# Stage 0 of a mixer layer: v first, phi folded in 64x64 tiles, and fp32 work gathered in shared runs

## The chip, the cores and the metric

The kernel runs on one core of a Trainium2 chip. The metric is the device time of one execution in microseconds; before the change it is 649.45 us, the median of three runs (648.33 to 650.24).

## What is computed

Input x is 2048 rows of 512. With xn = layernorm(x), the output is x + A(xn) + B(xn).

```python
# A: linear attention, 32 heads of 16
q, k, v = split(xn @ wqkv)
pq, pk = q @ w_phi[h], k @ w_phi[h]                      # per head
phi_q = concat(softmax(pq), softmax(-pq)); phi_k likewise
kv = phi_k^T v;  z = sum_s phi_k
A = (phi_q kv / (phi_q z + 1e-6)) @ wo
# B: gated MLP with a mix over the rows
z1, z2 = split(gelu(xn @ w_in)); z2 = layernorm(z2)
B = (z1 * (w_sp @ z2 + b_sp)) @ w_out
```

## The kernel before

Rows are taken in 16 tiles of 128 (NT). Stage 0, the first third of the time, makes k's features and the kv sum, q's features (sent to DRAM) and most of z1 before its gelu (sent to DRAM). Stage 1 makes z2, then comes w_sp @ z2, then the output projections. Only stage 0 is touched.

Most matmuls take fp32 data split in a high and a low part, both of a reduced fp32 format ("fp32r"): `mm3` (L49) issues high x high, high x low and low x high, at L51, L52 and L53. `round_h` (L41, ScalarE) makes the high part and `rest_l` (L46, VectorE) the low part. A projection of a tile to 512 columns is 12 such matmuls (`proj`, L213), z1 of a tile 24 of 344 columns (`zproj`, L122). Other matmuls run in plain fp32, and each is two records in the profile: the transposes of x (L248, one record each), the fold (L197) and the kv sum (L273).

The fold replaces q's and k's weights by their product with w_phi, so that a projection gives pq or pk straight away. `phi_bd` is w_phi as four block-diagonal 128x128 matrices (eight heads each). `fold` (L194) multiplies each 128x128 block of the transposed weights with it; `folded` (L201) splits the result into `wqk_h` and `wqk_l`.

Per tile s, stage 0 does this. `stats` (L232) takes mean and variance on VectorE, and POOL derives the rest. `center` (L241, ScalarE) subtracts the mean, `transposed` and `split_x` (L244, L226) turn the tile and split it, giving `xT[s]`. `proj_k` (L260) projects, and `softmax_pair` (L100) makes both softmaxes: two reductions (max, min), two subtractions, an exponential on ScalarE, a sum and a reciprocal. `add_kv` (L267) normalises the features on VectorE, adds them into `zacc` by a DMA, and multiplies them with v into one PSUM bank (16 matmuls on column tiles of 32, L271 to L274). `proj_v` (L255) and `proj_q` (L263) are the other projections; q lags by some tiles, and z1 (`z1_raw`, L136) by more.

What sets the order: the framework's planner orders each engine's instructions at build time, by its own estimate of when each is ready, earlier-written ones first. `tc.issue_after(i)` keeps the instructions that are written inside it, on i's engine, behind i. In the head (L296 to L339) `keep` puts nearly all into a fixed order: a table load and eleven idle transposes, statistics of tile 0, fold of k, splits of k's weights and of v's, k of tile 0, v of tile 0, fold of q in two halves. The loop (L341 to L357) is left to the planner. SP issues the loads in the order written (L276 to L282); x tiles go through five buffers (`XB`), and so do the eight pieces of w1 (`load_win`, L208).

Of the kernel before, what the change touches and what calls it, by code (L numbers as in the profile page):

```python
# [35 lines left out]
def mixer(ctx: ExitStack, tc: tile.TileContext, x, x_t, wv, wqkT, phi_bd, wo, w_in, wst, b_r, w_out, out):  # L36
# [63 lines left out]
    def softmax_pair(pl, src, tag, scale=1.0, ebufs=2):  # L100

        mm = pl.tile([P, 2, H], F32, tag=tag + "mm", bufs=1, name="mm")
        dve.tensor_reduce(mm[:, 0], heads(src), axis=AX.X, op=ALU.max)
# [4 lines left out]
        dve.tensor_tensor(e2[:, :, 0], heads(src), bc(mm[:, 0], H), op=ALU.subtract)  # L108
        dve.tensor_tensor(e2[:, :, 1], bc(mm[:, 1], H), heads(src), op=ALU.subtract)  # L109
        act.activation(e, e, AF.Exp, scale=scale)  # L110
        sm = pl.tile([P, 2 * H], F32, tag=tag + "sm", bufs=1, name="sm")
        dve.tensor_reduce(sm, heads(e), axis=AX.X, op=ALU.add)  # L112
        dve.reciprocal(r, sm)
        return er
# [7 lines left out]
    def zproj(ps, s, w, order=(0, 1)):  # L122
# [7 lines left out]
        for k, j in enumerate(order):  # L130
            for c in range(ND):
                cs = slice(c * P, (c + 1) * P)
                mm3(p[k][:, :FC], (t[:, 0, cs], t[:, 1, cs]), (w[j][0][:, c], w[j][1][:, c]), c == 0, c == ND - 1)
# [7 lines left out]

    LAG = 5
    xT = []
# [17 lines left out]
    with ExitStack() as p0:  # L161
# [16 lines left out]
        def split_w(h, l, src, t):  # L178
            sp.dma_start(t, src)
            round_h(act, h, t)  # L180
            rest_l(l, t, h)

        bd = stage("bd")[:, 0, :D]

        def load_rows(src, x_at={}):
            raw = [stage("wrow") for _ in range(2)]
            parts = [raw[c // 2][:, c % 2, :D] for c in range(ND)]
            for c in range(ND):
                if c in x_at:
                    fetch(x_at[c])  # L190
                sp.dma_start(parts[c], src[c * P:(c + 1) * P, :])
            return parts

        def fold(wT, g, accs):  # L194
            gs = slice(g * P, (g + 1) * P)
            for c, acc in accs:
                ins = pe.matmul(acc[:, gs], wT[g][:, c * P:(c + 1) * P], bd[:, gs], start=g == 0, stop=g == NG - 1,  # L197
                                skip_group_check=True).ins
            return ins

        def folded(i, accs, keep=lambda **ins: None):  # L201
            for c, acc in accs:
                keep(act=round_h(act, wqk_h[:, i, c], acc))
                keep(dve=rest_l(wqk_l[:, i, c], acc, wqk_h[:, i, c]))

        w1 = [[w1_pool.tile([P, ND, FC], F32R, name=f"w1_{j}{k}") for k in "hl"] for j in range(2)]

        def load_win(dst, j, stp, tag, bufs):  # L208
            for c in range(ND):
                t = stp.tile([P, D if tag == "x" else FC], F32, tag=tag, bufs=bufs, name="wst_")  # L210
                split_w(dst[0][:, c], dst[1][:, c], w_in[c * P:(c + 1) * P, j * FC:(j + 1) * FC], t[:, :FC])

        def proj(s, wh, wl):  # L213
            p = ps.tile([P, D], F32, tag="mm", name="proj")
            for c in range(ND):
                cs = slice(c * P, (c + 1) * P)
                proj.last = mm3(p, (xT[s][:, 0, cs], xT[s][:, 1, cs]), (wh[:, c], wl[:, c]), c == 0, c == ND - 1)
# [14 lines left out]
        def stats(s):  # L232
            st6 = wk.tile([P, 6], F32, tag="st6", name="st6")
            dve.bn_stats(st6, xt[s])
            nm = wk.tile([P, 1], F32, tag="nm", name="nm")
            ins = dve.bn_aggr(mv_x[:, s], st6).ins
            pool.tensor_scalar_mul(nm, mv_x[:, s, 0:1], -1.0)
            rstd_of(mv_x[:, s], r_x[:, s:s + 1])
            return nm, ins

        def center(s, nm):  # L241
            return act.activation(xt[s], xt[s], AF.Identity, bias=nm).ins
# [8 lines left out]
        def centered(s):  # L251
            center(s, stats(s)[0])
            split_x(transposed(s)[0])

        def proj_v(s):  # L255
            v[s] = wk.tile([P, D], F32, tag="v", name="v")
            ins = act.activation(v[s], proj(s, wv_h, wv_l), AF.Copy, scale=r_x[:, s:s + 1]).ins
            return proj.last, ins

        def proj_k(s):  # L260
            return softmax_pair(wk, proj(s, wqk_h[:, 1], wqk_l[:, 1]), "k", r_x[:, s:s + 1])
# [5 lines left out]
        def add_kv(s, er):  # L267
            vs, e = v.pop(s), er[:, :NF]
            dve.tensor_tensor(heads(e), heads(e), bc(er[:, NF:], 2 * H), op=ALU.mult)
            pool.dma_start(zacc, e, accum_op=ALU.add)  # L270
            for m in range(H // 2):  # L271
                k = m % 4 * QP
                pe.matmul(kv_acc[k:k + QP, m // 4], vs[:, m * QP:(m + 1) * QP], e[:, m * HP:(m + 1) * HP],  # L273
                          start=s == 0 and m < 4, stop=s == NT - 1, skip_group_check=True)  # L274

        sp.dma_start(bd, phi_bd.rearrange("p g f -> p (g f)"))  # L276
# [12 lines left out]
        def warm_up(n):  # L289

            t = ps.tile([P, ND, P], F32, tag="mm", name="idle")
            for k in range(n):
                i = pe.transpose(t[:, k % ND], ident, ident).ins
            keep(pe=i)

        with ExitStack() as queue:  # L296
            tbl = wk.tile([P, 1], F32, tag="nm", name="tbl")
            keep(act=act.activation(tbl, mhalf, AF.Identity, bias=mhalf).ins)
            warm_up(11)
            nm, i = stats(0)  # L300
            keep(dve=i, act=center(0, nm))
            accs = [(c, (za, kv_ps_p)[c // 2].tile([P, D], F32, tag="z", name="fold")) for c in range(ND)]
            for g in range(NG):
                if g == NG - 1:
                    pt, i = transposed(0)
                    keep(pe=i)
                keep(pe=fold(wkT, g, accs))
            i, j = split_x(pt)
            keep(act=i, dve=j)
            nm, i = stats(1)  # L310
            keep(dve=i)
# [3 lines left out]
            keep(act=center(1, nm))  # L315
            for c in range(ND):
                keep(act=round_h(act, wv_h[:, c], wvr[c]))
                keep(dve=rest_l(wv_l[:, c], wvr[c], wv_h[:, c]))
            p = proj(0, wqk_h[:, 1], wqk_l[:, 1])
            keep(pe=proj.last)  # L320
            pt, i = transposed(1)
            keep(pe=i)
            i, j = split_x(pt)
            keep(act=i, dve=j)
            nm, i = stats(2)
            keep(dve=i, act=center(2, nm))
            ek = softmax_pair(wk, p, "k", r_x[:, 0:1])
            keep(pe=proj_v(0)[0])
            for k in range(2):
                accs = [(2 * k + m, za.tile([P, D], F32, tag="z", name="fold")) for m in range(2)]  # L330
                for g in range(NG):
                    i = fold(wqT, g, accs)
                folded(0, accs)
                if k == 0:
# [4 lines left out]
                    proj_v(1)  # L339
        n1 = nq = 0  # L340
        for s in range(NT):  # L341
            fetch(s + 4)
            er = proj_k(s) if s else ek
            if 0 < s < NT - 2:
                centered(s + 2)
            while nq < (s - 2) * NT // (NT - 3):
                proj_q(nq)
                nq += 1
            add_kv(s, er)
            if s + 2 < NT:  # L350
                proj_v(s + 2)
# [82 lines left out]
    with ExitStack() as p1:  # L434
# [27 lines left out]
        with ExitStack() as p1a:  # L462
            ta = p1a.enter_context(left("tmp1a", 1))
            for j in range(2):
                load_win(w2[j], 2 + j, ta, "st", 4)
# [406 lines left out]
```

## Time and profile before

| | us |
|---|---|
| median of 3 runs | 649.45 |
| profiled execution | 649.57 |
| its span, first to last instruction | 647.8 |
| TensorE (PE) busy | 638.2 |
| VectorE (DVE) busy | 509.5 |
| ScalarE (ACT) busy | 278.7 |
| POOL busy | 96.3 |

Rows of the profile start with the source line, the engine and the operation, then the tile written and those read, by the program's names, with shapes. In a timeline the first two numbers are the start and the length in microseconds, and neighbours of one kind are merged with their count (x16). Matmul lengths include the way through the array, so a busy TensorE can overlap itself: what a matmul costs is read from start to start. PEld is the loading of weights, which overlaps the matmuls.

### The profile page before, as it was taken

Reading aid. Unit: us, or ns where it says so; the run is one execution under the profiler, and the core shown is the slowest. Engines: PE = TensorE matmul, PEld = TensorE weight load, DVE = VectorE, ACT = ScalarE, POOL = GpSimd, SP = SyncE. Lnnn points to the kernel's source line nnn. Section 1 sums busy time; section 2 is a strip of 40 time slices with the busy share of each in tenths; the row PEclk is TensorE's granted clock in tenths of the full one; section 3 lists DMA queues with packets and bytes.
Section 4 is the critical chain, followed back from the end, with each engine's and each line's share of the span. In section 5 each row is a group of like instructions: output and inputs, shape, how many; then the busy total and the mean of one; then the engine's idle time right before and its main releaser. Section 6 shows DMA issues by size and latency. Waiting matters only on the chain.

```text
span 647.8 us, 11206 instructions
## 1 busy us (share of the span) xinstructions
PE 638.2 (99%) x4291; PEld 576.1 (89%) x4291; DVE 509.5 (79%) x922; ACT 278.7 (43%) x464; POOL 96.3 (15%) x185
## 2 busy tenths in 40 slices
PE   7999999999999999999999999999999899999997
PEld 6888888888888999999999999999999677888885
DVE  4988888898889579889978778678696498989521
ACT  5644344332333437887443434434353332323330
POOL 3332221101100104542010010110100000001000
PEclk9999999999999999999999999999999999999999
DMA  8265345533463951002453352544548677775620
GB/s 308 76 165 129 110 119 121 155 114 102 125 183 98 291 187 66 2 2 65 142 179 124 122 175 79 172 128 120 178 157 277 201 271 261 243 264 222 225 66 32
DMA packets 39077, 98.12 MB, mean 151 GB/s; under 512 B 4880, under 2 KB 7184, under 8 KB 39024
## 3 DMA queue, kind: packets, MB, share of 16 engines
q1 hardware_dynamic: 27824, 56.51, 27.4%
q0 software_dynamic: 8896, 35.26, 18.0%
q10 hardware_dynamic: 2304, 5.64, 2.3%
q8 instruction: 33, 0.54, 0.3%
q14 instruction: 20, 0.16, 0.1%
HBM read 56.24 MB, written 26.48 MB: 128 GB/s over the span
## 4 chain that ended last, share of the span: by engine, by line
PE 95%; DMA 2%; DVE 1%; SPq 1%; ACT 0%; issue 0%; POOL 0%; ACTq 0%; POOLq 0%
PE g L53 11%; PE g L52 11%; PE g L51 11%; PE proj L53 7%; PE proj L51 7%; PE proj L52 7%; PE zps L53 6%; PE zps L52 6%; PE zps L51 6%; PE pout L51 5%; PE pout L53 5%; PE pout L52 5%; PE po L765 2%; PE kvps L273 1%; PE ptq L751 1%; PE pt L248 1%
## 5 line engine op out<-in xcount | busy, mean ns | idle before, releaser
L53 PE MATMUL g<-B,A 128*128 128x344 f32 x448 | 143.3, 320 | 0.0
L52 PE MATMUL g<-B,A 128*128 128x344 f32 x448 | 143.2, 320 | 0.0
L51 PE MATMUL g<-B,A 128*128 128x344 f32 x448 | 143.2, 320 | 0.0
L53 PEld LDWEIGHTS g<-B,A 128*128 128x128 f32 x448 | 84.2, 188 | 0.0
L51 PEld LDWEIGHTS g<-B,A 128*128 128x128 f32 x448 | 84.2, 188 | 0.0
L52 PEld LDWEIGHTS g<-B,A 128*128 128x128 f32 x448 | 84.1, 188 | 0.0
L47 DVE TENSOR_TENSOR A<-S,A 128x512 fp32r<-128x512 f32 x64 | 43.8, 690 | 33.6 <-ACT A L43 32.7
L43 ACT ACTIVATE A<-S 128x512 fp32r<-128x512 f32 x64 | 40.1, 631 | 58.9 <-PE g L53 36.0
L110 ACT ACTIVATE e<-e,r_x 128x1024 f32<-128x1024 f32 x32 | 36.8, 1151 | 41.2 <-DVE e L109 40.4
L51 PE MATMUL proj<-wqk_h,xT 128*128 128x512 f32 x128 | 51.4, 401 | 0.3 <-ACT wqk_h L43 0.3
L52 PE MATMUL proj<-wqk_l,xT 128*128 128x512 f32 x128 | 50.5, 394 | 1.1 <-DVE wqk_l L47 1.1
L43 ACT ACTIVATE A<-wf 128x512 fp32r<-128x512 f32 x64 | 33.4, 522 | 40.6 <-PE g L53 39.7
L53 PE MATMUL proj<-wqk_h,xT 128*128 128x512 f32 x128 | 50.9, 397 | 0.0
L51 PE MATMUL zps<-w_0h,xT 128*128 128x344 f32 x128 | 41.8, 326 | 0.0
L112 DVE TENSOR_REDUCE sm<-e 128x64 f32<-128x1024 f32 x32 | 38.7, 1208 | 3.3 <-ACT e L110 3.3
L51 PE MATMUL zps<-w_1h,xT 128*128 128x344 f32 x128 | 41.0, 320 | 0.0
L53 PE MATMUL zps<-w_0h,xT 128*128 128x344 f32 x128 | 41.0, 321 | 0.0
L53 PE MATMUL zps<-w_1h,xT 128*128 128x344 f32 x128 | 41.0, 320 | 0.0
L52 PE MATMUL zps<-w_0l,xT 128*128 128x344 f32 x128 | 40.9, 320 | 0.0
L52 PE MATMUL zps<-w_1l,xT 128*128 128x344 f32 x128 | 40.9, 319 | 0.0
L47 DVE TENSOR_TENSOR A<-wf,A 128x512 fp32r<-128x512 f32 x64 | 35.5, 555 | 3.4 <-ACT A L43 3.0
L753 ACT ACTIVATE f<-ptq 128x512 f32<-128x512 f32 x32 | 16.5, 602 | 33.6 <-PE ptq L751 27.1
(194 smaller groups left out, 1429.2 us busy)
## 6 DMA issues: line engine op xcount, KB each, us to landing
wf<-in_wst SPq DMA_DIRECT2D x64, 256.0 KB, 3.3
e_d<-e POOLq DMA_DIRECT2D x16, 544.0 KB, 5.0
et<-e_d SPq DMA_DIRECT2D x16, 544.0 KB, 5.2
zacc<-e POOLq DMA_DIRECT2D x16, 512.0 KB, 5.3
er<-et POOLq DMA_DIRECT2D x12, 512.0 KB, 4.1
u_d<-z1t POOLq DMA_DIRECT2D x16, 368.0 KB, 4.1
u<-u_d SPq DMA_DIRECT2D x15, 368.0 KB, 4.6
z_d<-z1f ACTq DMA_DIRECT2D x16, 344.0 KB, 3.4
```

What stands on the lines that cost most here:

```text
L43: return act.activation(h, src, AF.Copy).ins
L47: return (eng or dve).tensor_tensor(l, src, h.bitcast(F32), op=ALU.subtract).ins
L51: pe.matmul(dst, ah, bh, start=start, stop=False)
L52: pe.matmul(dst, ah, bl, start=False, stop=False)
L53: return pe.matmul(dst, al, bh, start=False, stop=stop).ins
L110: act.activation(e, e, AF.Exp, scale=scale)
L112: dve.tensor_reduce(sm, heads(e), axis=AX.X, op=ALU.add)
L248: ins = pe.transpose(pt[:, c], xs[:, c * P:(c + 1) * P], ident).ins
L273: pe.matmul(kv_acc[k:k + QP, m // 4], vs[:, m * QP:(m + 1) * QP], e[:, m * HP:(m + 1) * HP], start=s == 0 and m < 4, stop=s == NT - 1, ski ...
L751: pe.transpose(pt[:, a, k].bitcast(F32R), src, ident_r)
L753: act.activation(f, pt.rearrange("p a k b -> p a (k b)"), AF.Copy)
L765: lasts[3] = pe.matmul(po[r][c * QP:(c + 1) * QP, j // NG], kvT[rows, j], fs[j // 2][rows, j % 2], start=True, stop=True).ins
```

## The change

SP's queue starts with tile 0 of x, then v's weights, tile 1, phi, k's rows, tile 2, q's rows, tiles 3 and 4, and w1 as four whole rows of 688 columns, which are no longer loaded through the x buffers. The warm-up is six (and later one) fp32 matmuls of a tile of ones of 256 columns that VectorE fills. Tiles 0 and 1 are centered on VectorE. The head does v of tile 0, then the fold of k, v of tile 1, k of tile 0. The first v and k projections take all terms with the high weights first (`rest_last`). The fold multiplies only the 64x64 blocks on the diagonal, in the four quadrants of the array, into two banks (one for each half of the rows of phi).

In the loop, normalising is taken out of `add_kv`. Statistics of tile s + 3 stand behind the subtractions of k(s) on VectorE. On even s, `run` transposes tiles s + 2 and s + 3 and does the kv sums of tiles s - 2 and s - 1 in one piece on TensorE. It stands behind all projections and z1 written so far, and all that is written later stands behind it.

```diff
@@ softmax_pair
+        softmax_pair.shifted = dve.tensor_tensor(e2[:, :, 1], bc(mm[:, 1], H), heads(src), op=ALU.subtract).ins
@@ zproj
+        ahead_of_run.append(ins)
@@ fold
-            for c, acc in accs:
-                ins = pe.matmul(acc[:, gs], wT[g][:, c * P:(c + 1) * P], bd[:, gs], start=g == 0, stop=g == NG - 1,
-                                skip_group_check=True).ins
+            for n, banks in accs:
+                for c in range(2):
+                    for m in range(2):
+                        for r in range(2):
+                            rows = slice(r * HP, (r + 1) * HP)
+                            w0, b0 = (2 * n + c) * P + m * HP, g * P + r * HP
+                            ins = pe.matmul(banks[r][m * HP:(m + 1) * HP, c, g], wT[g][rows, w0:w0 + HP],
+                                            bd[rows, b0:b0 + HP], start=g == 0 and c == 0, stop=g == NG - 1,
+                                            skip_group_check=True).ins
@@ proj
+            if rest_last:
+                terms = [(at(k, c), wh[:, c]) for k in range(2) for c in range(ND)] + [(at(0, c), wl[:, c]) for c in range(ND)]
+                for n, (a, b) in enumerate(terms):
+                    proj.last = pe.matmul(p, a, b, start=n == 0, stop=n == len(terms) - 1).ins
@@ new helpers
+        def centered_on_dve(s):
+            stats(s)
+            ins = dve.tensor_scalar(xt[s], xt[s], mv_x[:, s, 0:1], None, op0=ALU.subtract).ins
+            rstd_of(mv_x[:, s], r_x[:, s:s + 1])
+            return ins
+        def run(tiles, feats):
+            with ExitStack() as order:
+                for i in ahead_of_run:
+                    order.enter_context(tc.issue_after(i))
+                ahead_of_run.clear()
+                pts = []
+                for t in tiles:
+                    pt, i = transposed(t)
+                    pts.append(pt)
+                    order.enter_context(tc.issue_after(i))
+                for t, e in feats:
+                    i = add_kv(t, e)
+            for pt in pts:
+                split_x(pt)
+            return i
@@ loads
+        fetch(0)
+        wvr = load_rows(wv)
+        fetch(1)
         sp.dma_start(bd, phi_bd.rearrange("p g f -> p (g f)"))
-        wkT = load_rows(wqkT[D:], {2: 0})
-        wvr = load_rows(wv, {2: 1})
+        wkT = load_rows(wqkT[D:])
         fetch(2)
         wqT = load_rows(wqkT[:D])
         fetch(3)
+        fetch(4)
+        w1r = load_rows(w_in[:, :FH], FH)
@@ head (the order of TensorE)
+            warm_up(6)
+            keep(dve=centered_on_dve(0))
...
+            pt, i = transposed(0)
...
+            i, j = proj_v(0, True)
...
+            pt, i = transposed(1)
...
                 keep(pe=fold(wkT, g, accs))
...
+            keep(pe=proj_v(1)[0])
+            stats(2)
+            i = center(2)
...
+            p = proj(0, wqk_h[:, 1], wqk_l[:, 1], True)
@@ loop
+            feats.append((s, normalise(er)))
+            if s > 1:
+                ahead_of_run.append(proj_v(s)[0])
+            if s + 3 < NT:
+                with tc.issue_after(softmax_pair.shifted):
+                    stats(s + 3)
+                center(s + 3)
+                if s == 0:
+                    split_x(transposed(3)[0])
...
             if s == 1:
-                for j in range(2):
-                    load_win(w1[j], j, wk, "x", XB)
+                with tc.issue_after(q_parts["act"]), tc.issue_after(q_parts["dve"]):
+                    for c in range(ND):
+                        round_h(act, w1_hl[0][:, c], w1r[c])
+                        rest_l(w1_hl[1][:, c], w1r[c], w1_hl[0][:, c])
...
+            if s and s % 2 == 0:
+                last = run([t for t in (s + 2, s + 3) if t < NT], feats[:-1])
+                behind.close()
+                behind.enter_context(tc.issue_after(last))
+                del feats[:-1]
+        for t, e in feats:
+            add_kv(t, e)
+        behind.close()
```

More of the change, by code (lines that the diff above doesn't have):

```diff
@@ L213, in proj @@
[L213 to L217, printed above, removed]
+            for n, banks in accs:
+                h, l = (w[:, i, 2 * n:2 * n + 2].rearrange("p c (g r e) -> p c g r e", g=NG, r=2)
+                        for w in (wqk_h, wqk_l))
+                for r in range(2):
+                    keep(act=round_h(act, h[:, :, :, r], banks[r]))
+                for r in range(2):
+                    keep(dve=rest_l(l[:, :, :, r], banks[r], h[:, :, :, r]))
@@ L464, in mixer @@
             for j in range(2):
-                load_win(w2[j], 2 + j, ta, "st", 4)
+                load_win(w2[j], 2 + j, ta)
             for s in range(NT - LAG, NT):
```

137 lines of the change are left out of this document (68 added, 69 removed).

## Prediction

> **What bounds the kernel now.** I read the page first: how long the span is, and how much of it TensorE works.
>
> ```profile
> span 647.8 us, 11206 instructions
> PE 638.2 (99%) x4291; PEld 576.1 (89%) x4291; DVE 509.5 (79%) x922; ACT 278.7 (43%) x464; POOL 96.3 (15%) x185
> ```
>
> TensorE is busy 638.2 of 647.8 us, and nearly all of the rest lies in the head and at the end. So every microsecond of TensorE work that goes is worth a microsecond, as long as nothing makes TensorE wait instead. The change touches only stage 0 (the first 215 us), so I asked for its stretches (columns: busy us and instructions of each engine, granted clock, DMA share, GB/s):
>
> ```profile
> 3.60:12.00 8.40, 6.63 (x42) 5.43 (x40) 3.01 (x7) 3.52 (x7) 1.92 (x6) 1.00 1.02 369
> 12.00:48.00 36.00, 35.88 (x245) 30.40 (x246) 33.40 (x60) 22.33 (x38) 11.07 (x28) 1.00 0.53 147
> 48.00:214.00 166.00, 166.00 (x1202) 140.68 (x1200) 144.48 (x210) 61.90 (x78) 28.68 (x49) 1.00 0.46 126
> ```
>
> Up to 12 us the DMA engines are full and VectorE is nearly idle. From 12 to 48 us TensorE is busy 35.88 of 36, but VectorE (third pair) is busy 33.40 of 36: it is a close second. From 48 us on VectorE has slack, 144.48 of 166. That middle row decides this case. Then the timeline of TensorE in the head:
>
> ```profile
> 1.81 2.61 PE L293 MATMUL idle<-ident 128*128 128x128 f32 x11 [1.81 <-POOL ident masks.py:199]
> 4.37 2.63 PE L197 MATMUL fold<-bd,wrow 128*128 128x128 f32 x16
> 7.21 1.16 PE L197 MATMUL fold<-bd,wrow 128*128 128x128 f32 x8 [0.22 <-DMA wrow<-in_wqkT]
> 8.50 0.66 PE L248 MATMUL pt<-ident,xt 128*128 128x128 f32 x4
> 9.00 1.06 PE L197 MATMUL fold<-bd,wrow 128*128 128x128 f32 x8
> 10.34 0.49 PE L51 MATMUL proj<-wqk_h,xT 128*128 128x512 f32 x1 [0.28 <-ACT wqk_h L43]
> 11.96 0.50 PE L52 MATMUL proj<-wqk_l,xT 128*128 128x512 f32 x1 [1.14 <-DVE wqk_l L47]
> 17.82 1.95 PE L197 MATMUL fold<-bd,wrow 128*128 128x128 f32 x16
> ```
>
> Unbroken work begins at 11.96 us. By then TensorE has done the k fold, four transposes and one projection matmul. Sixteen fold records at full clock take 1.95 us with 0.16 of pipeline tail, 1.8 us of TensorE, so the k fold's 32 are worth 3.6. With 0.44 and 0.23 (rows below) that is 4.3 us of work, and **7.7 us are lost** before 11.96. After it practically none are. So I compare lost time after the change with 7.7, less the work that the change saves.
>
> **What it saves: fp32 runs.** The features are multiplied into the kv sum once a tile. One such block, and one set of transposes, between their neighbours:
>
> ```profile
> 51.06 0.40 PE L53 MATMUL proj<-wqk_h,xT 128*128 128x512 f32 x1
> 51.39 0.65 PE L273 MATMUL kvps<-e,v 128*32 128x64 f32 x32
> 51.98 0.51 PE L51 MATMUL proj<-wv_h,xT 128*128 128x512 f32 x1
> 52.32 0.39 PE L52 MATMUL proj<-wv_l,xT 128*128 128x512 f32 x1
> 52.55 0.39 PE L53 MATMUL proj<-wv_h,xT 128*128 128x512 f32 x1
> ...
> 47.85 0.39 PE L53 MATMUL proj<-wqk_h,xT 128*128 128x512 f32 x1
> 48.08 0.60 PE L248 MATMUL pt<-ident,xt 128*128 128x128 f32 x4
> 48.44 0.47 PE L51 MATMUL proj<-wqk_h,xT 128*128 128x512 f32 x1
> 48.75 0.39 PE L52 MATMUL proj<-wqk_l,xT 128*128 128x512 f32 x1
> ```
>
> and the group of all kv records up to 215 us (busy, mean ns of one):
>
> ```profile
> L273 PE MATMUL kvps<-e,v 128*32 128x64 f32 x512 | 10.5, 222 | 0.0
> ```
>
> A projection matmul costs 0.23 us (52.32 to 52.55). From 51.06 to 52.32 are 1.26 us for two of them and the block, so the block costs 0.80. Its 32 records start within 0.65 less the length of the last, 0.22: 0.43 us, 14 ns each, with the last one's own some 0.45. The other 0.35 us are entering and leaving. Two kv blocks side by side pay them once, so eight pairs save 8 x 0.35, about **2.7 us**. For transposes, 47.85 to 48.75 are 0.90 us, less 0.46 is 0.44, or 0.11 each: no entry price, so putting eight together saves nothing.
>
> The Trainium skill (TensorEngine Tiling (Array Packing), Key Properties) says that changing the tiling mode drains TensorE. The trace agrees: the kv block, in column tiles of 32, pays 0.35 us at its ends, and the untiled transposes pay nothing.
>
> **The fold in 64x64 tiles.** No 64x64 matmul is in this trace. Each fold (k, q) becomes 64 calls, two records each, 64 columns long. The kv records, also 64 columns long and in tiles, cost 14 ns: 128 x 14 = 1.8 us a fold, against 3.6 now. If four tiles did not overlap but two, it is 28 ns and 3.6 us, no saving; if all four overlapped in both records, half, 0.9 us. I take 14 ns, the nearest row: **3.6 us** saved over both folds. Together 6.3 us.
>
> **What it moves: the head.** SP's queue now starts with tile 0 of x, and v's weights follow.
>
> ```profile
> bd<-in_phi_bd SPq DMA_DIRECT2D x1, 256.0 KB, 2.8
> 0.79 0.39 SPq L276 DMA_DIRECT2D bd<-in_phi_bd  x1
> ```
>
> The first transfer, issued at 0.79, lands 2.8 us later, at 3.6. At 369 GB/s the next 256 KB land every 0.7: wv by 6.4, tile 1 at 7.1, phi at 7.8, the k rows by 10.7, the q rows by 14.3, tiles 3 and 4 by 15.7, w1 (four rows of 344 KB) by 19.6. All of that is early enough not to be on the path behind the k fold. VectorE's prices come from its timeline:
>
> ```profile
> 10.44 0.68 DVE L234 BATCH_NORM_STATS2 st<-xt 128x6 f32<-128x512 f32 x1
> 11.15 0.18 DVE L236 BATCH_NORM_AGGREGATE mv_x<-st 128x2 f32<-128x6 f32 x1
> 11.25 2.45 DVE L47 TENSOR_TENSOR wqk_l<-fold,wqk_h 128x512 fp32r<-128x512 f32 x4
> 11.76 0.72 ACT L242 ACTIVATE xt<-xt,nm 128x512 f32<-128x512 f32 x1
> ...
> 24.58 1.21 DVE L112 TENSOR_REDUCE sm<-e 128x64 f32<-128x1024 f32 x1
> 25.71 0.51 DVE L47 TENSOR_TENSOR w_0l<-wst__439,w_0h 128x344 fp32r<-128x344 f32 x1
> 26.13 0.54 DVE L113 RECIPROCAL e<-sm 128x64 f32<-128x64 f32 x1
> 26.59 0.68 DVE L103 TENSOR_REDUCE mm<-proj 128x32 f32<-128x512 f32 x1
> ...
> 28.21 1.22 DVE L269 TENSOR_TENSOR e<-e 128x1024 f32<-128x1024 f32 x1
> 29.35 0.69 DVE L108 TENSOR_TENSOR e<-proj,mm 128x512 f32<-128x512 f32 x1
> ```
>
> From start to start: an operation on 512 columns 0.6 us, the softmax sum 1.13, a reciprocal 0.46, the normalising product 1.14, a rest on 344 columns 0.42 (so about 0.78 on 688), statistics of a tile 0.8 with their aggregate. Centering on VectorE isn't in the trace; by the 512-column row 0.6. Walking on: tile 0 is centered at 5.1, transposed by 5.7, split by 6.5; v of tile 0 runs from 6.5 to 9.9 (2.8 us of matmuls, the rest waits for weights being split); tile 1's transposes, 10.3; the k fold, 12.1; v of tile 1, 14.8; k of tile 0, 17.6. TensorE is at unbroken work at about 10 us with 3.2 us done: 6.8 lost, 0.9 better than now.
>
> **What it adds: the first run's wait.** On TensorE nothing written after a run may pass it, and the run must come after all projections named ahead of it. The first run (tiles 4 and 5, kv of 0 and 1) stands at s = 2. Ahead of it TensorE has only: transposes of five tiles 2.2, three v and three k projections 6 x 2.76 = 16.6, the folds 3.6, z1 of tile 0:
>
> ```profile
> 54.86 0.32 PE L53 MATMUL zps<-w_0h,xT 128*128 128x344 f32 x1
> ...
> 56.27 0.32 PE L53 MATMUL zps<-w_0h,xT 128*128 128x344 f32 x1
> ```
>
> These are nine matmuls apart, 0.157 each; 24 of them are 3.8. In all **26.2 us**, done at about 33 us if nothing stops it. VectorE, from the moment k of tile 0 is there (17.7 us), must first do: softmax of k0 and k1 2 x 4.0 (four times 0.6, 1.13, 0.46), four rests of the q fold 2.4, rests of x tiles 2 and 3 1.2, statistics of tiles 3, 4 and 5 2.4, two normalising products 2.3, four rests of w1 3.1, and the four maxima and subtractions of k2 2.4, behind which the diff pins the statistics of tile 5. Sum 21.8: 39.5 us. VectorE's short waits for ScalarE and TensorE add by the busy row of 12 to 48 us between 0 and 2.6; I take 0.6. From the aggregate to the end of centering on POOL and ScalarE the rows give 12.48 - 11.15 = 1.3. So **the transposes of tile 5 start at about 41.4 us**, and 41.4 - 26.2 = 15.2 us are lost then: 7.5 more than now.
>
> Behind those transposes on TensorE stand the two kv blocks and every later projection and z1; VectorE and ScalarE wait for the next k behind them. Before, TensorE filled this stretch with later v and k projections and with z1, because nothing fenced them off. That is how it stays busy there although VectorE is just as late.
>
> **Sum**: 7.5 lost more, 6.3 saved: +1.2 us. Break-even is a start at 40.2 us. Afterwards VectorE is 87% busy (144.48 of 166), 88% with 2.7 us less of TensorE, so I put the later runs at no wait. At nothing I also put w1 loaded whole (four rests of 0.78 against eight of 0.42, 0.25 us less of VectorE), rounding on ScalarE (busy 22.33 of 36), and the order of the rest parts; the cover is that ScalarE is free. The warm-up on ones has to bring the clock up by 6 us, as it came up within the first fold now; if it comes 2 us late, the v projection of tile 0 pays up to 1 us, most of it hidden behind the split weights.
>
> The profiled run took 649.57 us, 1.77 outside the span, and stands 0.12 over the median of 649.45. So the forecast is 649.45 + 1.2 = **650.7 us**. With the start of tile 5's transposes between 39.9 (no VectorE waits, tile 5's statistics not last) and 43.0 (waits as now), 649.1 to 652.3.
>
> **The rivals.** *The clock falls in the wait.* TensorE stands some 8 us, broken only by z1 of tile 0 and tile 4's transposes. At the end of the kernel the rows show what a long stand does:
>
> ```profile
> 643.58 0.39 PE L53 MATMUL pout<-woh,oT 128*128 128x512 f32 x1
> ...
> 646.00:647.00 1.00, 0.00 (x0) 0.00 (x0) 0.00 (x0) 0.00 (x0) 0.00 (x0) 1.00 0.25 92
> 647.00:647.80 0.80, 0.00 (x0) 0.00 (x0) 0.00 (x0) 0.00 (x0) 0.00 (x0) 0.71 0.00 0
> ```
>
> The last matmul ends at 643.97, and the clock falls to half in the last window, 3 to 3.5 us later (0.71 over 0.8 us is half from about 647.3). How long it takes to come back the head shows: the warm-up from 1.81 runs at 0.24 a transpose, against 0.11 later, and the first sixteen fold records take 2.63 us against 1.95, so six or seven of them are slow still, to about 5.7: 3.9 us. If one piece of the wait exceeds 3.3 us, about half of 3.9 us is lost: +1.9, 652.6 us, slower. For it: two pieces near 3.4 us come out of my tally. [...] The Trainium skill (TensorE: Matmul & The Clock Gate, Part 1) gives the rule that an idle window of about 3.4 us halves the clock and a busy one of the same length restores it; the rows here agree.
>
> *Later runs wait too.* From the end of k(s) to the run TensorE has a v, a q and a z1, 2.8 + 2.8 + 3.8 = 9.4 us; VectorE needs 2.4 + 0.8 and then 1.3 of centering for tile s + 3. It decides once more than some 4.9 us stand ahead of that on VectorE, one q softmax and a product (5.1). Six runs at 0.7 us give +4.2 and 654.9 us.
>
> *The 64x64 tiles do not overlap.* 28 ns a record: the saving is gone, and VectorE starts k0 1.8 us later: 653 us.
>
> *The wait is short.* VectorE stands idle some 5 us before 17.7 in my tally (for transposes, the fold, k0). If the fold is quicker and the planner fills that, tile 5 starts at 37.5: 3.6 lost more, 6.3 saved, 646.7 us, faster.
>
> **How the numbers follow.** Forecast as it stands 0.32; clock 0.24; short wait 0.26; later runs 0.11; fold 0.07. About 0.3% (2 us) is what a measurement of this kernel can tell from no change. Faster by more than that: nearly all of the short wait, 0.25. Within: the greater part of the forecast's own case (649.1 to 651.4) and a little of the short wait, 0.28. Slower: the rest, 0.47. The range 646.0 to 654.0 leaves out the best part of the short wait and most of the later runs' case, under 0.2.
>
> **What would show it.** Right: TensorE idle in pieces of some microseconds between 28 and 42 us, ended by ScalarE's centering of tile 5 or VectorE's rests of w1, and VectorE full from 18 to 40; kv records in groups of 64 every two tiles; fold records 14 ns apart. Wrong: TensorE at 9 or more from 12 to 48 us, or tile 5's transposes before 40 us. A granted clock of 0.5 behind 35 us is the first rival.

## The result, and the profile after

The changed kernel takes 657.99 us (median of 6 runs, 654.24 to 659.44) against 649.67 for the kernel before (6 runs, 647.58 to 651.17): a ratio of 1.012, with a 95% interval of 1.0082 to 1.0158. It is slower, by some 8 us where +1.2 was forecast, and above the range. The profiled execution took 659.44 us, 9.87 more than that of before. Its page:

```profile
span 657.7 us, 11569 instructions
PE 641.2 (97%) x4486; PEld 579.8 (88%) x4486; DVE 510.4 (78%) x921; ACT 275.6 (42%) x458; POOL 96.9 (15%) x183
...
PE   9879999999999999999999999999999899999997
PEclk9789999999999999999999999999999999999999
```

TensorE is now busy 641.2 of 657.7 us. It stands for 16.5 us instead of 9.6, and although the change takes work away, it is busy 3.0 us longer. The second and third slices (16.4 to 49.3 us) show both: TensorE at 8 and 7 tenths, and the granted clock at 7 and 8. The stretches, with the columns of the prediction (busy us and records of PE, PEld, DVE, ACT, POOL, granted clock, DMA share, GB/s):

```profile
12.00:48.00 36.00, 29.59 (x380) 24.65 (x380) 27.88 (x44) 18.04 (x29) 6.87 (x14) 0.85 0.44 136
48.00:214.00 166.00, 163.41 (x1191) 139.37 (x1184) 139.91 (x209) 59.86 (x79) 30.16 (x57) 0.99 0.45 125
```

From 12 to 48 us TensorE stands 6.41 us, where it stood 0.12. The clock is 0.85 on average, where it was 1.00. From 48 us on it stands 2.59 us, where it never stood. VectorE did not get fuller: 27.88 busy, where it had 33.40. It waits too. The timeline of TensorE (start, length, idle time before and its releaser in brackets):

```profile
1.24 5.49 PE L335 MATMUL idle<-warm 128*128 128x256 f32 x12 [1.24 <-DVE warm L348]
6.52 0.71 PE L268 MATMUL pt<-ident,xt 128*128 128x128 f32 x4
...
11.84 2.09 PE L206 MATMUL fold<-bd,wrow 64*64 64x64 f32 x128
13.87 0.51 PE L51 MATMUL proj<-wv_h,xT 128*128 128x512 f32 x1
...
20.70 0.66 PE L268 MATMUL pt<-ident,xt 128*128 128x128 f32 x4
23.65 1.87 PE L206 MATMUL fold<-bd,wrow 64*64 64x64 f32 x32 [2.29 <-DVE wqk_l L47]
...
27.22 0.63 PE L53 MATMUL proj<-wqk_h,xT 128*128 128x512 f32 x1
27.65 0.63 PE L51 MATMUL proj<-wqk_h,xT 128*128 128x512 f32 x1
...
41.66 0.60 PE L268 MATMUL pt<-ident,xt 128*128 128x128 f32 x4
46.37 1.12 PE L268 MATMUL pt<-ident,xt 128*128 128x128 f32 x4 [4.12 <-ACT xt L256]
```

Behind the warm-up the head runs nearly unbroken, then there are two waits. At 21.4 us the second half of the q fold waits 2.3 us: its two PSUM banks still hold the first half, until VectorE has taken the rest `wqk_l` from them. At 42.3 us the first run waits 4.1 us for tile 5 to be centered. Behind each wait the matmuls are slow: 0.43 us from start to start (27.22 to 27.65) instead of 0.23. Windows cut at the steps of the granted clock (the column behind POOL's), with the 3.41 us ahead of each fall apart, show why:

```profile
20.40:23.81 3.41, 1.12 (x36) 0.81 (x27) 3.38 (x8) 2.17 (x4) 0.46 (x3) 1.00 0.35 92
23.81:30.64 6.83, 6.83 (x51) 5.38 (x51) 4.99 (x7) 2.35 (x5) 1.63 (x2) 0.50 0.28 66
30.64:40.88 10.24, 10.24 (x79) 9.01 (x76) 8.59 (x14) 5.19 (x8) 0.31 (x2) 1.00 0.18 35
40.88:44.29 3.41, 1.37 (x10) 1.14 (x9) 3.41 (x7) 3.16 (x5) 0.71 (x2) 1.00 0.25 22
44.29:51.12 6.83, 4.75 (x72) 3.90 (x73) 4.69 (x6) 1.32 (x2) 2.72 (x4) 0.50 0.68 156
```

Twice a stretch of 3.41 us in which TensorE is busy only 1.12 or 1.37 us ends with the clock at half, and twice it stays there for 6.83 us. Of the 6.83 and 4.75 us of matmuls done at half clock, half is lost: 3.4 + 2.4 = 5.8 us.

The steps lie 6.83, 13.65 and 6.83 us apart, multiples of 3.41. The Trainium skill (TensorE: Matmul & The Clock Gate, Part 1) says that a free-running window of 3413 ns decides. The trace agrees with the step. It differs on the condition, an idle window for a fall and a busy one for the return: the windows here were a third busy when the clock fell, and it came back after two windows although the first was full. The measurement decides. One full window can be enough all the same: in run 6 below a second fall, at 68.91 us, lasts 3.41 us.

The later waits are two, at 122 and 175 us, 1.30 us each. All engines, around the first:

```profile
121.36 0.12 DVE L250 BATCH_NORM_AGGREGATE mv_x<-st 128x2 f32<-128x6 f32 x1
122.00 0.54 POOL L281 DMA_DIRECT2D e_d<-e  x1 [5.60 <-ACT e L110]
122.61 0.24 POOL L254 TENSOR_SCALAR nm<-mv_x 128x1 f32<-128x1 f32 x1
123.24 0.71 ACT L256 ACTIVATE xt<-xt,nm 128x512 f32<-128x512 f32 x1
124.01 0.65 PE L268 MATMUL pt<-ident,xt 128*128 128x128 f32 x4 [1.30 <-ACT xt L256]
```

The statistics are there at 121.5, but POOL negates the mean only at 122.61: ahead of it in its queue stands the issue of q's features to DRAM, which waits for the softmax. Centering, transposes and the run behind them wait for that.

**The account.** Rows before and after, in us of TensorE up to 214 us:

| | forecast | measured |
|---|---|---|
| fp32 work saved (kv pairs 2.7, folds 3.6) | -6.3 | -6.3 taken over |
| head, up to 12 us | -0.9 | +1.4 |
| standing from 12 to 48 us | +8.4 | +6.3 |
| standing from 48 us on | 0 | +2.6 |
| clock at half | 0 | +5.8 |
| sum | +1.2 | +9.8 |

Forecast in the third row are the 7.5 us lost more and the 0.9 won in the head. The head measured is 3.5 us more of warm-up matmuls less 2.1 us of standing. The sum fits the span, 9.9 us longer, so the savings can't be far from those taken over. Of the 8.6 us between the two sums, the clock is 5.8, the later runs 2.6 and the head 2.3; the standing up to 48 us came out 2.1 smaller than forecast.

### The profile page after: what moved, and what is told of

Same layout as the page of the kernel before. It is cut to its first block, busy times and chain, and to the rows that moved or that the text cites. A ratio compares the mean times of both kernels' runs of the same rounds, so it can differ in the third digit from the quotient of the medians.

```text
span 657.7 us, 11569 instructions
## 1 busy us (share of the span) xinstructions
PE 641.2 (97%) x4486; PEld 579.8 (88%) x4486; DVE 510.4 (78%) x921; ACT 275.6 (42%) x458; POOL 96.9 (15%) x183
## 4 chain that ended last, share of the span: by engine, by line
PE 95%; DVE 2%; DMA 1%; issue 1%; ACT 1%; POOL 0%; SPq 0%; DVEq 0%; POOLq 0%
PE g L51 10%; PE g L53 10%; PE g L52 10%; PE proj L51 7%; PE proj L53 6%; PE proj L52 6%; PE zps L51 6%; PE zps L53 6%; PE zps L52 6%; PE pout L51 5%; PE pout L53 5%; PE pout L52 5%; PE po L835 1%; PE ptq L821 1%; PE kvps L293 1%; PE pt L268 1%
## 5 line engine op out<-in xcount | busy, mean ns | idle before, releaser
L51 PE MATMUL proj<-wqk_h,xT 128*128 128x512 f32 x124 | 50.9, 410 | 0.0
L53 PE MATMUL proj<-wqk_h,xT 128*128 128x512 f32 x124 | 49.7, 401 | 0.0
L51 PE MATMUL zps<-w_h,xT 128*128 128x344 f32 x128 | 41.3, 324 | 0.0
L52 PE MATMUL zps<-w_l,xT 128*128 128x344 f32 x128 | 40.8, 318 | 0.0
L53 PE MATMUL zps<-w_h,xT 128*128 128x344 f32 x128 | 40.7, 320 | 0.0
L140 ACT ACTIVATE z1f<-zps,r_x 128x344 f32<-128x344 f32 (+1 forms) x29 | 16.4, 574 | 36.4 <-PE zps L53 36.3
L103 DVE TENSOR_REDUCE mm<-proj 128x32 f32<-128x512 f32 x32 | 22.0, 686 | 12.4 <-PE proj L53 10.0
L51 PE MATMUL pout<-wu,uh 128*128 128x512 f32 x75 | 30.7, 410 | 0.0
```

The source lines that it names most:

```text
L51: pe.matmul(dst, ah, bh, start=start, stop=False)
L52: pe.matmul(dst, ah, bl, start=False, stop=False)
L53: return pe.matmul(dst, al, bh, start=False, stop=stop).ins
L140: act.activation(z[:, k], p, AF.Copy, scale=r_x[:, s:s + 1])
```

## The experiments

The theory: VectorE is late in the first 40 us, as it was before. The two waits come from work that TensorE may not pass (the fold in the head's fixed order, then the run and the fence behind it), and the clock makes them dearer. The rivals: the runs cost time by themselves, the 64x64 fold does, or the first run only comes too early. Each edit is to the changed kernel unless said otherwise.

**1. k of tile 1 between the halves of the q fold**, to give TensorE work while the banks come free:

```diff
                     split_x(pt)
+                    p1 = proj(1, wqk_h[:, 1], wqk_l[:, 1])
+                    keep(pe=proj.last)
...
-            er = proj_k(s) if s else ek
+            er = proj_k(s) if s > 1 else softmax_pair(wk, p1, "k", r_x[:, 1:2], 3) if s else ek
```

> The changed kernel with the k projection of tile 1 placed ahead of the second half of the q fold, which stood 2.3 us for its PSUM banks at 21 to 24 us. Theory (waits of TensorE in the order, and the clock that falls behind them): the fold no longer waits, the clock stays at full from 24 to 31 us, VectorE does not stand from 29 to 32 us, and the transposes of tile 5 start at 41 to 43 us instead of 46.4; 652 to 655 us. Rival (VectorE's work ahead of the first run alone sets it): tile 5 still starts at 45 us or later and the time stays within 1.5 us of the changed kernel, 656.5 to 659.5 us.

654.04 us (653.53 to 655.24), ratio 1.0073 (1.0056 to 1.009). The fold's wait and the first fall of the clock are gone, and tile 5's transposes start 4.4 us earlier, but the run still waits and the clock falls behind it:

```profile
41.98 1.12 PE L268 MATMUL pt<-ident,xt 128*128 128x128 f32 x4 [4.18 <-ACT xt L256]
```

```profile
39.27:46.10 6.83, 4.12 (x71) 3.43 (x72) 5.32 (x8) 1.58 (x3) 2.72 (x4) 0.50 0.67 149
```

So the first wait with its fall is worth 3 to 4 us (4.0 by the medians, 3.1 by the two ratios), as the theory said.

**2. The same with idle matmuls in the run's wait.** They leave the run where it is and keep the clock up:

```diff
             pt = ps.tile([P, ND, P], F32, tag="mm", name="pt")
+            for k in range(14 if s == 5 else 0):
+                pe.matmul(pt[:, k % ND], ones, ones, start=True, stop=True)
```

> As the run before, and 14 fp32 matmuls on ones (28 records, 3.1 us at full clock) are put into tile 5's bank just ahead of its transposes, where TensorE waits anyway; they compute nothing that is used. Theory (the clock is a loss of its own, apart from the wait): the clock stays at full behind the first run and the time is 1.5 to 2.5 us under the run before. Rival (the wait is the whole loss): no gain over the run before, up to 1 us more.

652.33 us (651.98 to 652.58), ratio 1.0044 (1.0029 to 1.0059), 1.7 less than run 1.

```profile
38.07 3.29 PE L268 MATMUL pt<-ones 128*128 128x128 f32 x28
42.41 0.66 PE L270 MATMUL pt<-ident,xt 128*128 128x128 f32 x4 [1.05 <-ACT xt L256]
```

```profile
39.00:46.00 7.00, 5.95 (x99) 5.16 (x98) 6.03 (x9) 2.29 (x3) 2.73 (x4) 1.00 0.61 147
```

The transposes start no earlier (42.41 against 41.98), nothing useful was done in between, and the time falls all the same: the 1.7 us are the clock alone.

**3. The changed head without any runs**: transposes, kv sums and v as the loop had them before.

```diff
-                with tc.issue_after(softmax_pair.shifted):
-                    stats(s + 3)
+                stats(s + 3)
                 center(s + 3)
-                if s == 0:
-                    split_x(transposed(3)[0])
+                split_x(transposed(s + 3)[0])
...
+            add_kv(s, normalise(er))
+            if s + 2 < NT:
+                proj_v(s + 2)
...
-            if s and s % 2 == 0:
-                last = run([t for t in (s + 2, s + 3) if t < NT], feats[:-1])
-                behind.close()
-                behind.enter_context(tc.issue_after(last))
-                del feats[:-1]
```

> The changed head with the loop as before: transposes and the kv sum tile by tile, no run and no fence. Theory (the fences of the runs cost their waits, 4.3 + 2 x 1.5 us, and the clock behind the first, 2.4): 657.99 - 9.7 + 2.7 for the kv blocks apart again, about 651 us, with the wait of the q fold and one fall of the clock left in the head. Rival (the new head is the loss): 655 us or more.

658.01 us (656.09 to 658.33), ratio 1.0123 (1.0101 to 1.0146): no better than the change. I had expected 651, so the theory missed: the fold's wait grows. The first row is from the list of waits (sum, count, longest), the second from VectorE's timeline.

```profile
PE fold L206 <- DVE wqk_l L47: 5.6, 1, 5.6
```

```profile
21.77 0.70 DVE L249 BATCH_NORM_STATS2 st<-xt 128x6 f32<-128x512 f32 x1 [2.91 <-DMA xt<-in_x]
```

```profile
27.41:34.04 6.63, 6.63 (x43) 5.54 (x44) 6.34 (x11) 2.32 (x5) 0.88 (x1) 0.50 0.00 0
```

It is 5.6 us in one piece, and the clock is at half from 23.8 to 34.0. The edit did more than take the runs away: it also lets go of the statistics, which the change pins behind the subtractions. VectorE now takes them first, stands 2.91 us for a tile of x to land, and comes to the maxima of k0 at 23.41 us instead of 19.72; ScalarE centers three tiles before it rounds the first half of the fold, at 26.05 instead of 20.82. So the rests that free the banks come later too, and this run doesn't price the runs or the head alone. It shows that a fold in a fixed place on TensorE pays for what VectorE and ScalarE do ahead of its rests.

**4. The first run one step later**, at s = 4, the tiles before it singly:

```diff
-                if s == 0:
-                    split_x(transposed(3)[0])
+                if s < 3:
+                    split_x(transposed(s + 3)[0])
...
-            if s and s % 2 == 0:
+            if s == 2:
+                for t, e in feats[:-1]:
+                    add_kv(t, e)
+                del feats[:-1]
+            if s > 2 and s % 2 == 0:
```

> The changed kernel with its first run at s = 4 in place of s = 2: tiles 4 and 5 are transposed, and kv of tiles 0 and 1 summed, one by one and unfenced. Theory (only the first run meets VectorE's late start; later ones wait little): 4.3 us of wait and 2.4 of clock go, 650.5 to 652.5 us. Rival (a fence waits wherever it first stands): a wait of some 4 us at the run of s = 4, 656 us or more.

658.25 us (655.49 to 660.22), ratio 1.0132 (1.0099 to 1.0165), another miss. By the waits (sum, count, longest):

```profile
PE pt L268 <- ACT xt L256: 5.8, 4, 3.0
PE zps L52 <- DVE w_l L47: 2.6, 2, 1.4
```

The wait was moved, not removed: the run at s = 4 (64.2 us) waits 3.0 us, and z1 waits 2.6 for w1's rests. That the run only comes too early is refuted.

The fold's wait of 2.3 us is here as well (20.31 to 22.61), yet the clock stays up in this execution, of 655.49 us. Counted back from its fall behind the last matmul, at 653.02, this execution's steps of 3.41 us pass through 18.14 and 21.56, so the wait is shared by two windows:

```profile
18.14:21.56 3.42, 2.18 (x71) 1.50 (x69) 2.88 (x5) 1.14 (x3) 0.00 (x0) 1.00 0.60 192
21.56:24.97 3.41, 2.14 (x39) 1.92 (x40) 3.38 (x7) 3.15 (x6) 1.02 (x3) 1.00 0.23 64
```

In the change the same wait lay within one window, of 1.12 us busy. Here, then, what the clock adds to a short wait hangs on where it falls in that grid.

**5 and 6. Runs 3 and 4 with k of tile 1 ahead**, the edit of run 1 on top of each.

> The run without any runs or fences (e3_no_runs), with the k projection of tile 1 ahead of the second half of the q fold. In e3_no_runs the second half stood 5.6 us for its banks and the clock fell for 10.2 us. Theory (the loss of the head is that bank wait and the clock behind it; the rest of the head is a gain: folds 3.6 us less, about 0.9 less lost before 12 us): 645 to 647 us, faster than the kernel before. Rival (VectorE is too late for this head whatever the order): new waits of TensorE of 4 us or more between 20 and 50 us, 649.5 us or more.

> The kernel with the first run at s = 4 (e4_late_runs), with the k projection of tile 1 ahead of the second half of the q fold. Theory (fence waits are left only at s = 4, 3.2 us, and twice 1.5 us later): 650 to 652 us. Rival (the fences cost more than their waits, because they bind the order): 653 us or more.

655.8 us (653.78 to 657.32), ratio 1.0095 (1.0074 to 1.0117), and 657.72 us (656.83 to 660.65), ratio 1.0135 (1.011 to 1.0159). The theory had 645 to 647 and 650 to 652, so both missed. Waits of run 5, then of run 6:

```profile
PE fold L206 <- DVE wqk_l L47: 3.6, 2, 2.6
```

```profile
PE pt L268 <- ACT xt L256: 5.6, 3, 3.0
...
PE zps L51 <- DVE wqk_l L47: 2.3, 1, 2.3
PE kvps L293 <- DVE e L285: 1.8, 1, 1.8
```

With each edit another of VectorE's products is the late one (the fold's rests, the features, q's weights), and in both kernels the clock fell around 30 us, in run 6 again at 68.91. Run 5 has the statistics let go as in run 3, and VectorE comes to the maxima of k0 at 23.35. A cure that moves one wait doesn't help. The theory of one bad place was too narrow.

**7. Run 2 with q's features issued by SP instead of POOL:**

```diff
-            pool.dma_start(e_d[s], e)
+            sp.dma_start(e_d[s], e)
```

> The kernel e2_k1_first_filled (652.3 us) with the store of q's features issued by SP's queue in place of POOL's. In the two later runs that wait 1.5 us, tile s + 3's centering waits for POOL, which stands ahead of it at that store until q's reciprocal is done. Theory (POOL's order makes those waits): both go, about 2.9 us less, 649 to 650 us. Rival (VectorE's order makes them: the statistics stand behind the subtractions): the waits stay, 652 us or more.

649.82 us (649.29 to 652.5, 10 runs), ratio 1.0005 (0.9994 to 1.0017), 2.5 less than run 2. The two later waits (2.6 us) are gone: from 48 to 206 us TensorE is busy all of the time again. So those were POOL's queue and not VectorE's load, as the rows at 122 us say.

**8. The 64x64 folds alone in the kernel before.** `fold`, `folded` and `fold_banks` as in the change, nothing else:

```diff
-            accs = [(c, (za, kv_ps_p)[c // 2].tile([P, D], F32, tag="z", name="fold")) for c in range(ND)]
+            accs = [fold_banks(pl, n) for n, pl in enumerate((za, kv_ps_p))]
...
-                accs = [(2 * k + m, za.tile([P, D], F32, tag="z", name="fold")) for m in range(2)]
+                accs = [fold_banks(za, k)]
```

> The kernel before with one part of the change alone: both folds in 64x64 tiles, with the two-bank splits. Theory (14 ns a record): 3.6 us less work of TensorE, of which the k fold's 1.8 is partly lost in the head to the loads of k's rows; 646 to 648 us. Rival (the fold's time is hidden by VectorE's splits, which come after it in either form): within 1 us of the kernel before.

654.13 us (653.5 to 654.5), ratio 1.0071 (1.0056 to 1.0086): 4.4 slower, with 3 to 3.6 us less work. Both expectations missed. In this head the quicker fold has to wait 1.27 us for its weights to land:

```profile
5.04:8.45 3.41, 1.71 (x84) 1.30 (x76) 0.88 (x2) 0.42 (x1) 0.55 (x3) 1.00 0.97 344
8.45:18.69 10.24, 8.34 (x51) 6.19 (x52) 6.25 (x11) 5.64 (x11) 1.50 (x4) 0.50 0.76 281
```

The DMA engines are full (0.97), TensorE is busy half of a window, and the clock falls for 10.24 us: half of the 8.34 us worked in it, 4.2 us, is lost. From 12 to 48 us TensorE also stands 3.2 us (busy 32.82 of 36), where it stood 0.12. In the kernel before, with the slower fold, TensorE was busy 6.63 of the 8.40 us up to 12 us, and the clock stayed up.

**9. No fence behind the runs**: run 7 without its idle matmuls and without one line.

```diff
-            for k in range(14 if s == 5 else 0):
-                pe.matmul(pt[:, k % ND], ones, ones, start=True, stop=True)
...
-                behind.enter_context(tc.issue_after(last))
```

> e7_k1_filled_sp (649.8 us) without the idle matmuls ahead of tile 5, and without the one fence that keeps what is written after a run behind it; all else of the runs stays. The planner now puts one and a half z1 of the next tiles (36 matmuls, 5.6 us) between the transposes of tiles 4 and 5. Theory (the fence made the wait; TensorE had work but could not reach it): the 4.3 us of the first run's wait are filled and the clock stays: 645 to 646.5 us, faster than the kernel before. Rival (VectorE limits the start of stage 0 whatever TensorE does ahead): the wait comes back within the next 20 us, 648.5 us or more.

**646.73 us** (645.39 to 649.35, 12 runs), ratio 0.9964 (0.9949 to 0.9978): faster than both kernels, just above the 645 to 646.5 expected. The span is 644.3 us. TensorE's timeline:

```profile
37.04 0.66 PE L268 MATMUL pt<-ident,xt 128*128 128x128 f32 x4 [0.29 <-ACT xt L256]
...
43.24 0.60 PE L268 MATMUL pt<-ident,xt 128*128 128x128 f32 x4
```

Tile 5's transposes start later than in runs 1, 2 and 7 (43.24 against 41.98 to 42.41), but without a wait: between tile 4's and tile 5's TensorE now does 36 matmuls of z1. The run need not be early; what matters is that other work may go ahead of it.

**10. w1's rests on POOL**, in run 7's kernel, to take 3.1 us from VectorE:

```diff
-                with tc.issue_after(q_parts["act"]), tc.issue_after(q_parts["dve"]):
+                with tc.issue_after(q_parts["act"]):
...
-                        rest_l(w1_hl[1][:, c], w1r[c], w1_hl[0][:, c])
+                        rest_l(w1_hl[1][:, c], w1r[c], w1_hl[0][:, c], pool)
```

> e7_k1_filled_sp (649.8 us) with the four subtractions that make w1's low part on POOL in place of VectorE: 3.1 us less of VectorE ahead of the first run. Theory (VectorE's tally sets the start of tile 5's transposes): they start 2 to 3 us earlier than 42.4, and the time falls by 1.5 to 3 us, 647 to 648.3 us. Rival (ScalarE's and POOL's links set it, or POOL is too slow for w1: some 9 us of it): z1 of tile 0 waits instead, 650 us or more.

650.04 us (649.49 to 650.91), ratio 1.0007 (0.9997 to 1.0018): nothing won, and not conclusive. All engines, by start:

```profile
35.03 1.89 POOL L47 TENSOR_TENSOR w_l<-wrow,w_h 128x688 fp32r<-128x688 f32 x1
35.75 0.68 DVE L249 BATCH_NORM_STATS2 st<-xt 128x6 f32<-128x512 f32 x1
39.26 0.23 POOL L254 TENSOR_SCALAR nm<-mv_x 128x1 f32<-128x1 f32 x1
39.53 3.29 PE L268 MATMUL pt<-ones 128*128 128x128 f32 x28
42.66 0.60 PE L270 MATMUL pt<-ident,xt 128*128 128x128 f32 x4
```

VectorE does come to tile 5's statistics at 35.75, 2.8 us earlier than in run 7 (38.59). But POOL, at 1.89 us a rest, then holds the means of tiles 4 and 5, and the idle matmuls, which this kernel still has, hold the transposes. It shows that VectorE's tally can be eased, not what that is worth.

**11. The kv pairs alone in the kernel before**, with a fence, from s = 4 (seven pairs; `normalise` taken out of `add_kv`, more buffers for v and k):

```diff
-            add_kv(s, er)
+            feats.append((s, normalise(er)))
+            if s < 2:
+                add_kv(*feats.pop())
+            if s > 2 and s % 2 == 0:
+                with tc.issue_after(proj.last):
+                    for f in feats[:-1]:
+                        i = add_kv(*f)
+                behind.close()
+                behind.enter_context(tc.issue_after(i))
+                del feats[:-1]
```

> The kernel before with one part of the change alone: from tile 2 on, the kv sums of two tiles stand side by side, fenced, without transposes in the run; head, loads and the first two tiles as before. Theory (0.35 us a merge, seven merges, no wait because the features are long done): 2.4 us less, 646.5 to 648 us. Rival (any fence on TensorE's order costs what it saves): within 1 us of the kernel before or slower.

648.17 us (646.07 to 648.91, 12 runs), ratio 0.9976 (0.9964 to 0.9988): 0.8 to 2.3 us less, where 2.4 were worked out. One pair between its neighbours:

```profile
63.15 0.40 PE L54 MATMUL proj<-wqk_h,xT 128*128 128x512 f32 x1
63.48 1.10 PE L278 MATMUL kvps<-e,v 128*32 128x64 f32 x64
...
64.85 0.39 PE L53 MATMUL proj<-wv_l,xT 128*128 128x512 f32 x1
```

From 63.15 to 64.85 are 1.70 us, less 0.46 for two projection matmuls 1.24, against 2 x 0.80 for two blocks apart: 0.36 a pair, the forecast's 0.35. The profile shows no wait at this fence: no transposes stand in its run, and everything that the run needs is there. But it is of the fastest execution (646.07), and by the medians the gain is 1.0 us, not 2.4; what takes the rest is open.

**12. The change with only the fence behind the runs removed**, the one line of run 9:

```diff
-                behind.enter_context(tc.issue_after(last))
```

> The change as it is, with one edit: the fence that keeps what is written after a run behind it is left out; the q fold's second half still stands for its banks and POOL still stores q's features. Theory (the fence makes the run's waits, the banks and the clock behind them the rest): the 4.4 us at tile 5 are filled and the second fall of the clock goes, the 2.3 us at 21 us and the first fall stay: 650.5 to 653 us, some 5 to 7 us under the change. Rival (without the earlier k projection VectorE is still too late, and the wait moves to the next run): 655 us or more.

648.92 us (645.91 to 652.78, 12 runs), ratio 0.999 (0.9974 to 1.0006): 9.1 less than the change by the medians and 8.4 by the two ratios, with one line, and better than the 650.5 to 653 expected.

```profile
23.32:30.15 6.83, 6.74 (x45) 5.35 (x45) 5.24 (x8) 2.60 (x5) 1.80 (x3) 0.50 0.22 58
41.40:49.30 7.90, 7.90 (x111) 7.50 (x109) 7.09 (x11) 5.24 (x9) 2.73 (x5) 1.00 0.56 148
```

The fold's wait and the first fall are still there; the run's wait, the second fall and the later waits are not. Tile 5's transposes start at 47.66, later than in the change (46.37), and that costs nothing.

## Why the prediction was wrong, point by point

**Right, but for a small part: what is saved.** The k fold's 128 records take 2.03 us (11.84 to 13.87), 16 ns each where 14 were taken, so the two folds save about 3.1 us instead of 3.6. The kv pair saves 0.36 us. With either figure for the folds the account closes to half a microsecond.

**Right: VectorE's tally and the wait's mechanism.** From k of tile 0 on VectorE to the end of tile 5's aggregate the prediction had 21.8 us of work. In the trace:

```profile
19.72 0.69 DVE L103 TENSOR_REDUCE mm<-proj 128x32 f32<-128x512 f32 x1 [2.03 <-PE proj L229]
...
32.29 0.69 DVE L47 TENSOR_TENSOR wqk_l<-fold,wqk_h 128x512 fp32r<-128x512 f32 x1 [3.46 <-ACT wqk_h L43]
...
44.20 0.17 DVE L250 BATCH_NORM_AGGREGATE mv_x<-st 128x2 f32<-128x6 f32 x1
```

19.72 to 44.37 are 24.65 us, less 3.46 of standing 21.2. The list differs by two items, which make up most of the difference: one normalising product (1.14) comes only behind, at 44.29, and a third rest of x (0.6) stands in it. The run then waited for ScalarE's centering of tile 5, as forecast.

**Wrong: when that tally starts, and that it runs through.** The transposes were forecast at 41.4 and came at 46.37, 5.0 later. k of tile 0 reached VectorE 2.0 us late (19.72 instead of 17.7). The step "tile 0 is centered at 5.1, transposed by 5.7" has the centering right (4.95), but the transposes stand on TensorE behind the twelve warm-up records, until 6.52. The prediction gave the warm-up no length; its own 0.24 us for 128 columns at half clock makes 5.8 for twelve records of 256, and they took 5.3 (1.24 to 6.52). So the head, put at 0.9 us better, came out 1.4 worse. "I take 0.6" for VectorE's short waits was 3.46: there it waits for the last part of the q fold, which TensorE does late and at half clock. From the aggregate to the transposes it was 2.2 and not 1.3 us: POOL's negation took 1.03 us there.

**The step that failed** is the one that makes the first run's wait the only place where TensorE stands, at full clock: "26.2 us, done at about 33 us if nothing stops it". Something did: the second half of the q fold has to wait for the banks of the first. In the kernel before, the halves stand at 17.82 and 26.39 us, with transposes and v and k of tile 1 between them, and the second half waits for nothing:

```profile
26.39 1.95 PE L197 MATMUL fold<-bd,wrow 128*128 128x128 f32 x16
```

The change moves v ahead, and the prediction costed that move by its start alone, not by what it had covered. That wait of 2.3 us is short, but it brought the clock down for 6.83 us. TensorE was through with the work ahead of the run at 42.3 us and not at 33, so the run's wait is 4.1 us where 8.4 were forecast, and the loss sits in the head, the fold's wait and the clock instead.

**The first rival came true, twice and dearer.** It had the price at 1.9 us, for one piece over 3.3 us, and 3.9 us until the clock is back. In fact 2.3 us of standing was enough, the clock stays down 6.83 us, and the two falls cost 5.8 us. So the forecast's sum had the clock at nothing, and that is its largest miss. The rival's condition, one unbroken piece of 3.3 us, is too strict: what the rows show is a fixed grid of 3.41 us and how busy TensorE is in one of its stretches. Run 2 shows the price by itself, 1.7 us for one fall. How often the clock falls differs by execution: those of the change go from 654.24 us at a mean clock of 0.997 to 659.44 at 0.990. The two at 0.997 lost some 2 us by the clock (0.003 of their span) and are still 4.6 us and more above the median of the kernel before, so the waits cost time without the clock too.

**"I put the later runs at no wait"** missed 2.6 us: two of the six later runs wait 1.30 each. The rival for it named VectorE and six waits of 0.7, a figure that nothing in it works out. It was POOL's queue, which the prediction did not look at: the change makes the run wait for tile s + 3 just when q's features are sent off from the same queue (run 7).

**What the run's wait is made of** is settled by runs 9 and 12. VectorE is no earlier there: tile 5's transposes come at 43.24 and 47.66 us. The fence behind the run turns that into time, because it keeps z1 and projections that are ready from filling in. What runs or the head cost alone is open, because run 3 changed VectorE's order with them. That the size of VectorE's tally would set the time if it were eased was only argued: run 10 could not show it.

## What to carry to other kernels

When an order is fixed on an in-order engine, go through each instruction that is moved away and ask what it covered where it stood; then ask the same of each fence: what ready work may not pass. Fp32 work saved on the bounding engine is worth its time only where a wait doesn't take its place: the same folds cost 4.4 us in one head (run 8), and kv pairs gained in a stretch with slack (run 11). Price a wait on TensorE with what the clock does behind it, and cut the windows at the clock's steps to see it.

## What the runs showed of the hardware that was not expected

- The granted clock fell behind stretches of 3.41 us in which TensorE was busy 1.12 and 1.37 (the change), 1.21 (run 12), 1.55 (run 1), 1.41 (run 3), 1.34 (run 5), 1.59 and 0.98 (run 6) and 1.71 us (run 8): it need not stand for the whole of one. It stayed up behind 1.83 (run 5, 22.89 to 26.30), 2.00 (the kernel before, 9.04 to 12.45) and 2.14 (run 4), but also behind 1.58 (run 4, 65.93 to 69.34), so the busy share alone doesn't settle it.
- It came back after 3.41 us (run 6, from 68.91), 6.83 (most falls) or 10.24 (runs 3 and 8). What decides between them is open.
- POOL takes 1.89 us for a rest on 688 columns (run 10). VectorE takes 1.65 for two of them in the change (34.09 to 35.74).
